# A gated mix of two long convolutions: 640 matmuls that nobody reads near the start, and a new written-out order of all engines

## The chip, the cores and the metric

The kernel runs on one core of a Trainium2 chip. The metric is the device time of one execution in microseconds (us): the median of several runs. A profile of one execution comes with it, taken on the chip, with the start and the duration of every instruction.

## What is computed

Two sequence layers share the input `u` (2048 steps, 448 channels, bf16), and a gate mixes them.

```python
g = sigmoid((u * gate_w).sum(-1, keepdims=True))
K = einsum("dn,dnl,dn->dl", C, exp(dt * A * l), dt * B).real   # 256 complex modes per channel
a = irfft(rfft(u) * rfft(K)) + u * Dskip                       # layer A, length 4096, first 2048 kept
k_shift = sum over t of shifted k * shift_k[:, t]              # four taps
kv = k_shift * v
b = u * (irfft(rfft(kv) * rfft(ssm_k)) + kv * ssm_D)           # layer B
out = g * a + (1 - g) * b
```

## The kernel before

The Fourier transforms are done as matmuls. The 448 channels are worked in four groups of 112 (28 columns in each of four strips of partitions, `H` = 0 to 3), for the two layers A and B. A transform has three forward steps: `spread` (tiles `ps_c`, moved from PSUM into `zs` or `zsK`), `transform` (tiles `ps_2`, which the profile shows as `ps<-zs,s_W`, moved into the same tile), and two multiplications of spectra on VectorE (`products`, which write `zs` and `zsS`). Back again go `stage_a` (matmuls `ps_a` with the table `sa_R`, moved into `U`) and `stage_b` (matmuls `ps_b` with the table `sb_G`).

The kernel `K` of layer A is made on the chip, in eight blocks (class `KGen`, `block(j)` for j = 0 to 7). ScalarE makes powers of the modes (`Tables.levels` and `reals`: Exp and Sin into `ET`), one set for two blocks. VectorE multiplies them out into two tiles, `kg_TQ` and `kg_TP`. When these are complete, 224 small matmuls go into `pk`, and the copy `kg_S`, the gathering matmuls `ps_g`, the copy `kg_KT`, a `spread` and a `transform` follow. In all there are 5,387 matmuls, each with its own weight load.

PSUM holds three buffers under the tag `ps` for all of `ps_v`, `ps_m`, `ps_c`, `ps_2`, `ps_a` and `ps_b`, so a matmul group can start only when the group three before it has been moved out. The moves out are mostly ScalarE's (`evac`).

In the first 45 us the loads arrive, ScalarE and VectorE make the tables (`s_W`, `sb_G`, `sa_R`, `Wc`), and the four-tap sum of `k` runs in eight pieces: VectorE writes `kvt`, eight matmuls of 448 columns add up in `ps_v`, ScalarE copies to `kt`. `sa_R` comes from four phase rows on VectorE, one Sin on ScalarE, and one scaling on VectorE (`Consts.stage_a`).

What sets the order: `Order` records every engine call in program order without issuing it. `ORDER` is a written-out string of call numbers, and `Order.issue` issues the calls in that order, with an order-only dependency between neighbours on one engine. So the queue of each of the five engines, SyncE's DMA issues and GpSimd's index rows among them, is fixed by this string, and every instruction in the profile carries one line, L146. Readers of the profile go by tile names. Tiles are named below with their buffer numbers where several of a name must be told apart, such as `zsK_296`. They are the names in the built program.

Of the kernel before, what the change touches and what calls it, by code (L numbers as in the profile page):

```python
# [41 lines left out]
    "604 23 166 27 73 65 26 31 576 1 75 164 525 74 24 36 76 171 194 192 172-173 198 193 25 35 188 177 174-175 195 582 "  # L42
    "189 580 176 0 34 199 581 201 162 593 160 33 163 594 161 190 165 595 588 167 2 168 577 32 597 178 169 606 602 29 "
    "22 16 191 17 179 21 12 38 13-14 18-19 15 181 186 10 28 180 182 8 170 20 9 3 187 6 183 37 11 7 5 4 30 536 534 528 "
    "526 184 42 79 68 529 185 527 46 535 39 537 544 47 542 196 545 531 197 44 550 202 200 590 583 552 45 543 541 584 "
    "596 589 48 585 591 100 40 530 41 55 533 43 586 101-108 592 603 587 72 67 599 598 49 110 51-52 538 66 90 50 56 "
    "234-241 69 77 532 54 120 53 109 64 242 70 63 215-222 78 80 539 62 243-250 71 540 225-232 61 223 549 224 233 "
    "121-128 130 548 203 546 204 131-138 150 129 547 111-118 551 139-140 600 151-158 119 553 601 554 251 141-148 159 "
    "557 252-259 267 149 319-326 260 327 302-317 556 285-300 318 261 91-98 301 262 555 205-212 81-88 213 99 214 263 "
    "268-283 264 89 265 1110 284 266 574 367 474 346-353 575 366 1111 472 578 471 481 1108 365 354 1109 476 502 473 "  # L50
    "607 364 470 469 468 475 494 561 579 570 565 573 558 566 559 517 563 516 569 478 518 490 512 503 507 498 477 513 "
    "487 489 479 482 519 491 608-635 493 480 483 492 495 486 484 387-402 488 499 496 500 508 1126 522 497 501 485 521 "
    "504 524 370-385 523 514 2488 505 509 636-663 515 506 510 664-691 520 1124 511 1113 692-719 386 1127 1115 1114 "
    "1116 560 421-428 1122 1117 1120 567 403 1129 1119 562 820-835 1131 571-572 1118 720 568 1112 564 429 1852 1121 "
    "721 803-818 2495 2510 2489 2499 2491 1133 2493-2494 2496 1123 2492 722 2490 1135 337-344 836 57 60 59 58 723 "
    "1125 2497 1141 404-419 819 724 345 725 355-362 2511 2498 1137 420 786-801 605 1128 363 777-784 1138 802 328-335 "
    "1130 1140 785 743-758 336 1132 430-437 1142 759-775 1134 1143 438 1464-1479 776 1136 457-464 1851 1139 1853 2500 "
    "1272-1335 1854 1862 837-844 1855 1857 1336-1367 465 1208-1271 2501 2503 2502 845 1856 2504 1480 369 368 2505 "
    "2520 1481-1496 2519 2512 1858 1515-1522 2521 960-967 1859 1144-1207 2506 2513 2523 1497 2514 2522 2515 1861 968 "
    "2524 448-455 1860 2516 439-446 1368 1864 1863 456 1369-1385 2517 2508 2507 2518 1865 969-976 1867 1386 447 1866 "  # L60
    "1387-1426 1869 977 1868 942-949 466 1427 726-741 950 1446-1451 2525 1498-1513 1870 742 2526 1848 1872 1514 1849 "
    "467 924-931 1847 932 906-913 1846 2509 1874 914 863-878 2542 2529 1877 2527-2528 897-904 2543 1523 1875 879-895 "
    "2545 1876 905 933-940 2530 2544 915-922 2563 896 2534 2531 2537 2562 2532 2538 1662-1669 923 2564 1850 2533 2565 "
    "941 1871 1644-1651 1670 1460 951-958 2566 1873 2535 846-861 1461 2569 1652 2536 1878 959 2202-2217 862 2568 1880 "
    "2218 978-1041 1879 2539 1452 1881 2555 2949-2964 1453-1458 2540 2074-2105 1463 2554 2556 2550 1043-1106 "
    "2557-2558 1462 2561 2546 2541 1882-1945 1459 2965 1107 2552-2553 2549 1042 2559 1437-1444 2551 1584-1599 2560 "
    "2573 1445 2567 2548 2966-2981 2547 1600 1428-1435 6194 3968 1618-1633 1436 2570 2982 1653-1660 2571 1946-2009 "
    "1661 2572 2574 1634 2010-2073 2577 3976 3994 3973 3988 1635-1642 3974 3987 3971 2576 2219-2234 2579 3975 2575 "
    "3977 3332 2581 1643 1601-1616 3995 3972 2583 3970 2106 2585 2578 1524-1539 2235 2588 2580 1617 3331 2125-2164 "
    "3333-3334 1575-1582 3969 2165 2582 1558-1573 1583 1540 3335 2107-2123 2584 1541-1556 1574 3337 1671-1678 2590 "  # L70
    "2124 2236-2251 1557 3338 2184-2189 1679 2589 1716-1779 2190 2199 3336 2252 2166-2173 2198 2591 3996 2983-2998 "
    "3339 1707-1714 1780 2174 3997 3000-3007 2999 3982 3341 2191-2196 3983 1715 2586 1698-1705 2197 2253-2260 3340 "
    "3008 3984 2587 1689-1696 1706 3343 2175-2182 2592 2261 1680-1687 1697 2322-2329 4008 3346 2785-2816 1688 "
    "2721-2784 4009 3348 2330 3985 3350 2183 2201 2593-2656 2200 2920-2927 2349-2356 2928 2657-2720 2357 3352 3354 "
    "3342 4010 2262-2277 3357 3345 2817 3344 4011 3989 3347 2818-2834 4012 2340-2347 4023 2278 4000 2313-2320 3999 "
    "4022 2348 3349 3156-3163 4024-4025 3351 2321 1781-1844 3164 4043 3353 4001 4014 2835 4013 2938-2945 4002 4015 "
    "3060-3067 3978-3979 2946 1845 2836-2875 3980 3043-3058 3990-3991 3068 3981 3992 4004 4016 2279-2294 3986 4003 "
    "3993 4005 4018 4042 2296-2311 3998 3355 3059 4044 3356 2295 2331-2338 3358 2312 3026-3041 4045 2876 3360 "
    "2929-2936 2339 2895-2900 4006 3361 4007 2909 3682-3697 2937 4017 4046 2910 4019 3359 2358-2421 4029 4047 "
    "3426-3489 4038 4020 4040 4050 4039 4037 2422 4021 4041 3362-3425 4030 4049 4031 3042 4048 3554-3585 4053 4052 "  # L80
    "4026 4034 4051 4032 4027 6197 4036 4033 2911-2918 4035 3490-3553 4028 4054 2919 5388 4057 3699-3714 3698 4812 "
    "2948 3733-3740 3586 3715 3138-3145 3741 2947 3129-3136 3146 3009-3024 5395 5390 3716-3731 5397 5402 5394 4056 "
    "5410 2901 5403 3025 4055 4059 2902-2907 4058 2908 4811 3174-3181 3732 4060 2886-2893 5411 4813 4062 5391 "
    "2423-2486 3137 4061 5393 5396 4064 5389 3811-3818 4063 2894 4069 3182 2877-2884 5392 2487 3069-3084 3819 4814 "
    "2885 3147-3154 3085 4070 3120-3127 3587-3603 3155 4815 3192-3199 4071 3604 4818 4446-4461 3200 4065 4820 "
    "3605-3644 5404 4068 4817 3103-3118 4066 3645 5399 3128 5398 3655-3662 4067 5400 3086-3101 5405 3663 4072 3119 "
    "3671-3676 5407 4265-4296 4816 3102 4732-4747 3677 5401 5412 4819 3802-3809 4748 5408 3646-3653 5414 4073-4136 "
    "4822 4821 5406 5413 4462 3678-3679 4823 3829-3836 4201-4264 5415 3654 4826 3837 6200 3165-3172 3664-3669 5416 "
    "4137-4200 4828 3810 5429 4830 3173 5428 5417 4832 5418 3183-3190 4824 4297 4825 4766-4773 4827 3191 3201-3264 "
    "4829 4774 3681 3670 5409 3820-3827 3265 5424 4298-4314 5423 4749-4764 3680 4315 5425 4463-4478 3828 4765 "  # L90
    "4316-4355 5426 4831 4409-4416 4479 3266-3329 5419 4833 4356 5420 4417 4839 5421 4838 5458 4480-4487 4382-4387 "
    "5422 4429-4444 4840 5457 5443 5427 5442 5459 5444-5445 3330 5463 5462 4835 4488 4391-4398 4388-4390 3793-3800 "
    "5455 5464 4836 4399 4357-4364 4834 5460 4841 4418-4425 5461 4445 4837 5473 5034-5065 5452 5465 5447 4842-4905 "
    "4426 6195 4970-5033 5448 5466 5454 5433 4365 5468 5456 5469 5451 5450 5467 5453 5446 5449 4375-4380 4400-4407 "
    "5430 5434 5470 4715-4730 6196 4906-4969 4408 5431 5437-5438 4731 5475 3759-3774 4428 4381 5066 5439 4366-4373 "
    "4802-4809 5476 5435 4427 4374 4810 5085-5124 5432 3776-3791 5125 5850 5472 3801 5471 3775 5067-5083 4549-4556 "
    "5436 5474 5084 4506-4521 5440 4557 5477-5478 5441 5151-5156 3742-3757 5479 3792 5480 5849 5482 5157 4567-4574 "
    "3758 5135-5142 5851 5484 4575 3838-3901 5486 4522 5490 5143 4540-4547 3902 4523-4538 5487 4548 5481 5144-5149 "
# [533 lines left out]
def body(  # L632
# [20 lines left out]
    nc = Order(tc)  # L653
# [169 lines left out]
    V.tensor_scalar(out=sel_d[:], in0=dj[:], scalar1=0.0, scalar2=None, op0=ALU.is_equal)  # L823
    pk = psk.tile([P, 512], f32, name="pk")
    V.memset(pk[:], 0.0)

    kg = KGen(tc, nc, kgp, pk, psk, cons, sel_d, d4, ET)
    KA = [None] * NQG
    XA = [None] * NQG
# [168 lines left out]
```

## Time and profile before

| | |
|---|---|
| median of 7 runs | 295.63 us |
| range of the runs | 294.22 to 296.56 us |
| the profiled execution, its own time | 295.48 us |
| its span, first to last instruction | 293.2 us |
| mean granted TensorE clock | 0.891 |
| VectorE (DVE) busy | 265.4 us, 540 instructions |
| ScalarE (ACT) busy | 253.9 us, 411 instructions |
| TensorE (PE) busy | 212.1 us, 5,387 matmuls |
| GpSimd (POOL) busy | 7.4 us |
| moved by DMA | 21.34 MB |

The page gives, for each engine, busy time as a share of the span, then the span in 40 slices of 7.3 us with the busy share in tenths. PEclk is the TensorE clock that was granted, in tenths of full speed. "PEld" is the weight load of TensorE. In a list of waits, "A <- B" means that A stood idle until B released it, and "<- issue" is idle time for which no wait is recorded.

### The profile page before, as it was taken

To read this page: it belongs to the slowest core of one execution; us is meant where nothing else is said; L and a number is where in the kernel's file an instruction comes from. 1 tells how busy PE (TensorE), PEld (TensorE's weight loads), DVE (VectorE), ACT (ScalarE), POOL (GpSimd) and SP (SyncE) were. 2 spreads that over 40 slices of the span, in tenths; PEclk is the share of its full clock that TensorE was granted. 3 is DMA by queue.
4 is the path that set the end of the run, shared out by engine and by line. 5 is a ranking of instruction groups with operands and counts; after the bars stand their busy time and mean duration, and the time that the engine had idled before them with its cause. 6 is when DMAs were issued, how large, how long until landed. Compare 5 with 4: busy or idle time off the path is not lost.

```text
span 293.2 us, 12044 instructions
## 1 busy us (share of the span) xinstructions
PE 212.1 (72%) x5387; PEld 185.6 (63%) x5387; DVE 265.4 (91%) x540; ACT 253.9 (87%) x411; POOL 7.4 (3%) x43
## 2 busy tenths in 40 slices
PE   0067771658977798988998678879677998589740
PEld 0033451647766687877888568869577897578740
DVE  8998999999999989999999899889999999794950
ACT  4999899999999999999799999989999987537500
POOL 7000000000000100000000000000000000000000
PEclk9995995755988999997999799989799999799965
DMA  7999999340144232031004300320500046000068
GB/s 149 190 190 141 174 166 271 63 64 0 35 97 65 48 83 51 2 79 52 4 4 96 75 9 3 65 67 6 125 4 2 4 93 159 7 6 4 2 119 135
DMA packets 53380, 21.34 MB, mean 73 GB/s; under 512 B 48720, under 2 KB 51664, under 8 KB 53328
## 3 DMA queue, kind: packets, MB, share of 16 engines
q1 hardware_dynamic: 48768, 19.42, 36.1%
q10 hardware_dynamic: 4560, 1.15, 2.1%
q8 instruction: 42, 0.69, 1.0%
q14 instruction: 10, 0.08, 0.1%
HBM read 10.01 MB, written 3.21 MB: 45 GB/s over the span
## 4 chain that ended last, share of the span: by engine, by line
ACT 37%; DVE 21%; PE 17%; SPq 9%; issue 6%; DMA 5%; DVEq 0%; ACTq 0%
ACT zs L146 12%; ACT ET L146 9%; SPq L146 9%; DVE kg_P L146 6%; PE pk L146 5%; ACT zsK L146 4%; PE ps_b L146 4%; ACT U L146 3%; PE ps_a L146 3%; PE ps L146 3%; ACT L146 3%; ACT ks_mag L146 3%; DVE kg_TQ L146 3%; DVE zsS L146 3%; DVE ug L146 2%
## 5 line engine op out<-in xcount | busy, mean ns | idle before, releaser
L146 ACT CAST zs<-ps 128x896 bf16<-128x896 f32 x48 | 44.4, 960 | 0.3 <-PE ps L146 0.3
L146 ACT CAST zs<-ps_c 128x1024 bf16<-128x1024 f32 (+1 forms) x48 | 44.2, 942 | 0.0
L146 PEld LDWEIGHTS <-s_W 128*128 128x128 bf16 x544 | 31.9, 106 | 17.2 <-issue 13.7
L146 PE MATMUL pk<-kg_TP,kg_TQ 128*25 128x32 bf16 x1792 | 32.5, 239 | 6.7 <-issue 6.5
L146 DVE TENSOR_TENSOR kg_P<-kg_TQ,ET 128x896 bf16<-128x896 bf16 (+2 forms) x56 | 36.2, 654 | 0.5
L146 PE MATMUL ps<-zs,s_W 128*128 128x112 bf16 x384 | 29.4, 227 | 7.8 <-ACT zs L146 6.0
L146 PEld LDWEIGHTS <-kg_TQ 128*25 128x25 bf16 x1792 | 28.3, 128 | 9.5 <-issue 7.8
L146 PE MATMUL ps_a<-sa_R,zs 128*128 128x128 bf16 x224 | 32.3, 231 | 2.7 <-ACT zs L146 1.6
L146 PE MATMUL ps_b<-U,sb_G 128*128 128x28 bf16 x1024 | 28.3, 175 | 6.1 <-issue 2.6
L146 PEld LDWEIGHTS <-sb_G 128*128 128x128 bf16 x1024 | 27.3, 96 | 7.1 <-issue 4.4
L146 PE MATMUL ps_a<-sa_R,zsS 128*128 128x128 bf16 x224 | 31.6, 229 | 0.0
L146 ACT CAST U<-ps_a 128x1024 bf16<-128x1024 f32 (+2 forms) x30 | 28.0, 963 | 3.8 <-PE ps_a L146 3.8
L146 DVE TENSOR_TENSOR kg_P<-kg_TP,ET 128x1792 bf16<-128x1792 bf16 (+1 forms) x32 | 31.0, 970 | 0.1
L146 PEld LDWEIGHTS <-zsS 128*128 128x128 bf16 x224 | 29.4, 151 | 2.4 <-issue 2.2
L146 PEld LDWEIGHTS <-zs 128*128 128x128 bf16 x224 | 29.3, 151 | 1.8 <-DVE zs L146 0.5
L146 PE MATMUL ps_v<-kvt,scratch 128*128 128x448 bf16 x64 | 15.9, 411 | 16.2 <-DVE kvt L146 14.1
L146 ACT ACTIVATE ET<-ks_ph 128x448 bf16<-128x448 int16 x40 | 23.4, 609 | 0.7 <-DVE kg_P L146 0.7
L146 DVE TENSOR_TENSOR kg_TQ<-kg_P 128x448 bf16<-128x448 bf16 (+2 forms) x56 | 23.4, 420 | 0.1
L146 PE MATMUL ps_c<-Wc,kv 128*64 128x128 bf16 x224 | 17.3, 309 | 7.3 <-ACT zs L146 6.5
L146 PEld LDWEIGHTS <-scratch 128*128 128x128 bf16 x65 | 6.9, 110 | 23.7 <-issue 15.8
L146 PEld LDWEIGHTS <-kv 128*64 128x64 bf16 x224 | 16.0, 218 | 8.4 <-issue 7.5
L146 ACT CAST zsK<-ps_c 128x384 bf16<-128x384 f32 (+2 forms) x27 | 21.0, 779 | 0.0
(103 smaller groups left out, 458.5 us busy)
## 6 DMA issues: line engine op xcount, KB each, us to landing
zsS<-zs SPq DMA_DIRECT2D x16, 448.0 KB, 5.2
kt<-in_B_k_dram SPq DMA_DIRECT2D x16, 112.0 KB, 4.0
vt<-in_B_v_dram SPq DMA_DIRECT2D x4, 448.0 KB, 6.7
skraw<-in_B_ssm_k_dram SPq DMA_DIRECT2D x16, 112.0 KB, 3.6
uu<-in_A_u_dram SPq DMA_DIRECT2D x4, 448.0 KB, 8.8
xfd<-ks_hold SPq DMA_DIRECT2D x2, 672.0 KB, 5.1
ks_xf<-xfd SPq DMA_DIRECT2D x3, 336.0 KB, 3.2
out_dram<-ug SPq DMA_DIRECT2D x8, 112.0 KB, 4.3
```

What stands on the lines that cost most here:

```text
L146: ins = f(*args, **kw)
```

## The change

Part one adds matmuls behind the line that clears `pk`. Each multiplies 128 weight columns of `sa_R` with 64 other columns of it and writes the last 64 columns of the bank of `pk`, which nothing reads. There are 20 times 32 of them.

```diff
     pk = psk.tile([P, 512], f32, name="pk")
     V.memset(pk[:], 0.0)
 
+    for _ in range(20):
+        for i in range(32):
+            nc.tensor.matmul(pk[:, 448:512], lhsT=R[:, 0:128], rhs=R[:, 128:192], start=True, stop=True)
+
     kg = KGen(tc, nc, kgp, pk, psk, cons, sel_d, d4, ET)
```

Part two replaces the whole string `ORDER`. The new calls carry the numbers 605 to 1244 and stand in 40 groups of 16, some of them side by side. Every call behind them in program order has a number that is 640 higher than before. The beginning of the string, old and new:

```diff
-    "604 23 166 27 73 65 26 31 576 1 75 164 525 74 24 36 76 171 194 192 172-173 198 193 25 35 188 177 174-175 195 582 "
...
+    "604 26 525 34 23 27 198 190 576 164 25 33 2 1 166 73 24 36 11 194 10 192 186 8 195 0 35 9 193 187 12 196 14 188 "
...
+    "529 602 177 537 31 527 39 590 161 542 4 162 168 597 167 530 534 68 20 163 5 204 595 165 65 535 605-620 29 577 75 "
+    "169 552 581 541 38 171 550 170 621-636 172 42 582 173 603 175 583 540 174 76 41 584 178 637-652 43 653-668 543 "
...
```

In the built program the new matmuls stand on TensorE as 240 ahead of everything else, 48 behind the first `ps_m` group, 112 in five groups of 16 and one of 32 among the `ps_v`, `ps_m` and `ps_c` groups that follow, 160 behind the last `ps_c` group of the first spectrum, and 80 more two `ps_c` groups later, ahead of the 112 matmuls of the gate. No other instruction is added to TensorE, VectorE, GpSimd or SyncE. ScalarE has 15 loads of its function table where it had 13. The sequences of all five engines differ.

## Prediction

> **What bounds the kernel now.** I read the busy rows and slices of the page first, then the busy time by stretch, then each engine's timeline and the waits.
>
> ```profile
> PE 212.1 (72%) x5387; PEld 185.6 (63%) x5387; DVE 265.4 (91%) x540; ACT 253.9 (87%) x411; POOL 7.4 (3%) x43
> ...
> PE   0067771658977798988998678879677998589740
> ...
> DVE  8998999999999989999999899889999999794950
> ACT  4999899999999999999799999989999987537500
> ...
> PEclk9995995755988999997999799989799999799965
> ```
>
> ```profile
> 0.00:45.00 45.00, 22.44 (x177) 12.81 (x177) 41.81 (x99) 39.40 (x43) 5.70 (x40) 0.92 1.13 168
> 45.00:80.00 35.00, 21.60 (x488) 19.44 (x490) 33.95 (x88) 34.91 (x73) 0.87 (x2) 0.66 0.38 83
> ...
> 145.00:227.00 82.00, 67.62 (x1850) 61.71 (x1843) 77.82 (x157) 80.65 (x144) 0.00 (x0) 0.94 0.18 41
> 227.00:254.00 27.00, 22.95 (x729) 21.01 (x727) 27.00 (x48) 21.30 (x29) 0.00 (x0) 0.99 0.32 72
> 254.00:284.00 30.00, 23.59 (x755) 22.20 (x751) 21.74 (x29) 14.63 (x20) 0.00 (x0) 0.90 0.10 20
> ```
>
> The columns are the stretch, its length, and the busy time of PE, PEld, DVE, ACT and POOL, then clock, DMA share, GB/s. ACT is full from 45 to 227 us and DVE from 45 to 254. PE is not: from 45 to 80 us it runs at 0.66 of its clock and ACT still idles only 0.09 us. A colder or warmer PE there moves nothing. From 254 us on, no engine is full; a chain through PE, ACT and DVE runs.
>
> I took the time of each instruction from the timeline (start to end, or to the next start where two overlap) and added up each engine's work to any point; the idle time to that point is its clock time less this sum. The point that sets the end is the product on DVE that needs the last move into zsK_296: ACT has done 210.9 us of work at its end, at 219.9 us, so it has idled 9.0 us (3.9 before its first instruction, 1.6 up to 33 us, 3.5 later). DVE starts the product at 220.0 and works on, nearly without a gap, to the last kg_TP of the last block at 254.1: 34.0 us. So the path is 210.9 + 9.0 + 34.0 + 0.2 = 254.1, and the end is 39.1 us later, at 293.2.
>
> ```profile
> 14.14 3.15 PE L146 MATMUL ps_v<-kvt,scratch 128*128 128x448 bf16 x8 [14.14 <-DVE kvt L146]
> ...
> 40.07 1.67 PE L146 MATMUL ps_v<-kvt,scratch 128*128 128x448 bf16 x8 [0.21 <-ACT zs L146]
> ...
> 251.84 1.58 PE L146 MATMUL ps_b<-U,sb_G 128*128 128x28 bf16 x57 [2.58 <-issue]
> ...
> 260.36 1.16 PE L146 MATMUL pk<-kg_TP,kg_TQ 128*25 128x32 bf16 x63 [1.36 <-issue]
> ```
>
> ```profile
> q8 instruction: 42, 0.69, 1.0%
> ...
> L146 ACT ACT_TABLE_LOAD x13 | 16.7, 1283 | 4.0 <-DMA kt<-in_B_k_dram 3.9
> ```
>
> The same eight matmuls take 3.15 us on a cold PE and 1.67 us on a warm one. The pauses marked "issue" stand where an instruction packet lands: 0.69 MB in 42 packets for 10,774 weight loads and matmuls is 256 instructions to a packet.
>
> **What the skill says.** "TensorE: Matmul & The Clock Gate", Part 1, has PE at half clock until about 3.4 us of activity have passed; the halves of 3.15 and 1.67 us agree, and the clock row falls to 5 around each lull. "ScalarE: Activation LUTs", What ACT_TABLE_LOAD costs, gives 1283 ns and 1380 ns of drain: the trace has 1283 ns, and no drain, since ACT is busy again at once. "Runtime: NRT & Kernel Launch", Instruction fetch mechanics, has blocks of 256 instructions, fetched while the last one runs and mostly hidden; the packets agree, but 2.58 and 1.36 us at 249 and 259 us are not hidden.
>
> **The change, part by part.**
>
> *The 640 matmuls, price.* No row has 64 columns against 128 weight columns in bf16. From below, ps_b (28 columns) runs at 1.58/57, some 28 ns apiece. From above, transform's 112 columns start 50 ns apart on a warm PE and 94 on a cold one. I take 30 warm and 53 cold.
>
> *240 of them first.* They wait for sa_R, which the new order makes first: ACT's table load ends at 5.1, the Sin takes 0.4, and DVE's scaling is ready at about 6.5. With 3.4 to 6.8 us cold (64 to 128 matmuls) and the rest warm they end at 15 to 17 us. The first kvt, which they stand before, ends on DVE at 16: its place is 1.2 us later than before in DVE's work, and POOL now makes a 512-wide row (0.6 us), smaller ones and a clearing ahead of c_pidx, for which DVE waits some 0.75 us. ACT asks for the first ps_m at 19.5 and for the first ps_v at 22.6 (before: 20.3 and 19.6). So all 240 lie in idle PE time. If that cover fails, by half clock throughout (240 x 53 = 12.7) and a fetch pause of 2.6, PE is at 22 instead of 17 and ACT waits.
>
> *The other 400* stand before ps_h, ps_m and ps_c groups which wait for one of three PSUM buffers anyway; following buffer by buffer, only one wait is left, 0.8 us at the ps_v just before the last ps_c. The 160 end at 46.4 when kv is ready on DVE (46.2); the 80 end before gwt is. Nothing on the path.
>
> *What a warm PE saves.* Up to 45 us ACT lost 0.27 us to ps_v, 0.83 to DVE's sb_ph (itself behind 0.86 for ps_v) and 0.49 to s_ph. Against the 0.8 that remains I get ACT's second Exp load at 42.8 instead of 43.6: -0.8 us. Bounds: -1.7 (no wait) and +3 (cover gone).
>
> *Two more table loads.* ACT now changes to Sin and back within three instructions, after 105 us of its work, for the one phase tile ks_ph_293. 2 x 1.28 = +2.6 us on an engine that is full there. At the joint above, the work sums are: ACT to the last move into zsK_296 209.9 (before 210.9), DVE from there 37.2 (before 34.0), in all 247.1 against 244.9: +2.2 us. The earlier joint at zs_329 reads 246.9 against 244.2. These moves carry the table loads in them. Cover: ACT's 3.5 us of scattered waits after 33 us, if the order closes them. I take them as they are, since they stand by PE pauses and late phases that no order names. Bounds: -1.2 (all closed: 2.2 - 3.4) to +2.7.
>
> *SP and POOL.* The B_im and A_re loads come earlier, the last kt is 20th instead of 23rd, dB 32nd instead of 30th, d4 22nd; xfd moves ahead of the reload of skraw_193, and the last uu stays 41st. The readers of dB and uu (a ps_c group at 31 us, the gate at 50) wait for PSUM and gwt longer than for these. Zero; with the next DMA later, 1 us at most.
>
> *The tail.* The seventh block's kg_TQ is complete 2.4 us later in DVE's work, so its 224 pk matmuls end at about 246 instead of 242.8, if the last kg_TP is kept at 254.1. But 1280 instructions are five packets exactly, so packets now end at known matmuls: not inside the ps_b group that stood 2.58 us. Following PSUM buffers, the last pk group starts at 255.1 instead of 256.4, has 16 fewer transforms behind it, and loses the same 1.3 us to a packet: kg_S at 261.0 instead of 261.6. From there the new order of ps_a, ps_c and ps_b again needs 16.7 us to the last ps_b. So -0.5; bounds -2.6 (pause gone and nothing late) and +2.4 (the late kg_TQ in full).
>
> **Sum.** -0.8 + 2.2 - 0.5 = +0.9 us on the profiled execution: 295.48 + 0.9 = 296.4. Its own time is 0.15 under the median of 295.63, so I say 296.5. The span would be 294.1.
>
> **Rivals.**
>
> A: the new order closes ACT's waits. After 33 us these are 3.5 us; if 1 us is left and the tail brings 1 us instead of 0.5, the sum is 0.9 - 2.5 - 0.5 = -2.1, 293.5. It turns when ACT idles less than some 6.5 us up to the joint (9.0 now). For it: ACT and DVE are so nearly full that each order must be well balanced, and the late pause goes. Against it: 2.6 us more of ACT's work.
>
> B: nothing that can be measured. DVE's 265.4 us are the same, the new matmuls are hidden, and gains and losses cancel: 295.6. For it: the sum of parts is small. Against: every queue is permuted, and pauses of 1 to 3 us will fall elsewhere. About 0.3%, 0.9 us, is what a measurement of this kernel can tell from none.
>
> C: the front fails. The DMA engines are fullest in the first 15 us, and PE must fetch its second packet there. If the 240 stay cold and stand once, ps_v is 4 to 5 us late and ACT with it: 300. Against it: ACT has 2 us in hand.
>
> **Chances.** The forecast, slower by some 1 us, 0.40; A 0.37; B 0.15; C 0.08. The forecast's own spread (+0.2 to +3) puts part under 0.3%. Faster 0.38, same 0.18, slower 0.44. Its own range is 295.8 to 298.5. The whole: down to 291.5 (ACT's waits closed and the pause gone: 0.9 - 3.4 - 2.1 = -4.6), up to 300.5 (C).
>
> **What would show it.** PE starts near 6.5 us and is warm from 10 to 13 us; 240 matmuls end before 17. ACT's second Exp load starts near 42.8. 15 table loads of 1283 ns. The last kg_TP on DVE ends near 255, the last kg_S starts near 262. I am wrong if ACT's idle time up to its last zsK_296 move is under 7 us, or if PE has not begun ps_v by 18 us.

## The result and the profile after

The changed kernel takes 1.0074 times as long as before (95% interval 1.0054 to 1.0093), which is 2.2 us on 295.63, or 297.8 us. The ratio counts, for each kernel, only the executions within 1.5% of its fastest; the changed kernel spreads without a gap from 295.5 to 301.2 us, ten of its 27 runs fall outside, and the medians of all runs, 299.18 us beside 295.91, lie 3.3 us apart. The profiled execution takes 298.21 us, with a span of 296.0 (before: 293.2). So it is slower, as forecast, and 1.3 us above the 296.5 that I named.

The page of the changed kernel, in the lines that answer to those of before:

```profile
PE 229.6 (78%) x6027; PEld 205.2 (69%) x6027; DVE 266.1 (90%) x540; ACT 256.8 (87%) x413; POOL 9.9 (3%) x43
...
DVE  7999999999959999999999999899999999982960
ACT  3999999999979899999999999999999994927500
...
PEclk9999999956977799999999879998979997979985
...
q8 instruction: 47, 0.77, 1.1%
...
L150 PE MATMUL pk<-sa_R 128*128 128x64 bf16 x640 | 21.9, 197 | 7.8 <-DVE sa_R L150 7.5
...
L150 ACT ACT_TABLE_LOAD x15 | 19.2, 1283 | 4.1 <-DMA kt<-in_B_k_dram 3.9
```

PE has 17.5 us more work, ACT 2.9, DVE 0.7. The clock row starts full and the 640 matmuls cost 21.9 us of PE. ACT has 15 table loads of the same 1283 ns. The instruction queue (q8) has 47 packets instead of 42. The busy time by stretch (stretch, length, PE, PEld, DVE, ACT, POOL, clock, DMA share, GB/s) shows where it went wrong; the last line is of the kernel before:

```profile
0.00:45.00 45.00, 33.93 (x660) 26.40 (x661) 42.65 (x101) 39.28 (x42) 7.24 (x40) 1.00 1.06 157
...
80.00:145.00 65.00, 52.97 (x1427) 47.51 (x1427) 59.06 (x118) 62.22 (x104) 0.42 (x1) 0.92 0.21 44
```

```profile
80.00:145.00 65.00, 53.85 (x1411) 48.41 (x1407) 63.11 (x125) 63.04 (x107) 0.79 (x1) 0.95 0.26 56
```

Up to 45 us DVE and ACT have done about what they did before. From 80 to 145 us DVE is busy for 59.1 of 65 us; in the kernel before it was busy for 63.1. PE's front is as forecast (start, length, instructions, idle time before them and its releaser):

```profile
7.46 8.04 PE L150 MATMUL pk<-sa_R 128*128 128x64 bf16 x223 [7.46 <-DVE sa_R L150]
...
16.77 1.48 PE L150 MATMUL ps_v<-kvt,scratch 128*128 128x448 bf16 x7 [0.26 <-DVE kvt L150]
```

The 240 end at 16.5 us, and the first `ps_v` group runs warm at once. The loss is here, in the timeline of all engines:

```profile
77.04 1.66 PE L150 MATMUL pk<-kg_TP,kg_TQ 128*25 128x32 bf16 x95
...
82.18 1.67 PE L150 MATMUL pk<-kg_TP,kg_TQ 128*25 128x32 bf16 x97 [3.48 <-issue]
...
84.74 0.91 ACT L150 CAST zs<-ps 128x896 bf16<-128x896 f32 x1 [1.83 <-PE ps L150]
...
86.66 0.67 PE L150 MATMUL pk<-kg_TP,kg_TQ 128*25 128x32 bf16 x32
...
87.39 0.22 DVE L150 COPY kg_TP<-ET 128x224 bf16<-128x224 bf16 x1 [3.03 <-PE pk L150]
```

PE works through the 192 `pk` matmuls of block 0 and stands 3.48 us in the middle of them, with no wait recorded. Behind it ACT waits 1.83 us for a `ps` group, and DVE waits 3.03 us: `kg_TP` has one buffer, so its first write for block 1 must wait until the last 32 `pk` matmuls have read block 0. The trace says what PE stood for. Counted in order, PE's weight loads and matmuls show every pause of PE marked "issue" in both kernels right behind record 193 plus a multiple of 256, where a new instruction packet is needed. When PE enters the 256 instructions of one packet (128 matmuls), the next packet is asked for: that is read from the landings, most of which begin within 1.3 us of such a point. The packet that PE stood for was so asked for at 75.56 us; it begins to land at 79.51, 3.94 us later, and PE goes on 1.31 us after its last byte. In the kernel before, in block 0's `pk` matmuls, these waits were 0.73 and 0.62 us (75.21 to 75.95 and 78.80 to 79.42), and PE did not stand. There `ps_c` groups stand between the `pk` matmuls, and PE worked 3.6 us on a packet:

```profile
76.50 1.17 PE L146 MATMUL pk<-kg_TP,kg_TQ 128*25 128x32 bf16 x64
77.61 0.71 PE L146 MATMUL ps_c<-Wc,kv 128*64 128x128 bf16 x8
78.25 1.63 PE L146 MATMUL pk<-kg_TP,kg_TQ 128*25 128x32 bf16 x96
```

In the changed kernel the 192 stand in a row, and PE is through the packet entered at 75.56 us in 2.9 us. What delays the next packet is, by the times, the first swap, two DMAs of 448 KB. SyncE's issues, first of the kernel before, then of the changed one:

```profile
78.38 1.18 SPq L146 DMA_DIRECT2D zsS<-zs  x2
```

```profile
74.27 1.18 SPq L150 DMA_DIRECT2D zsS<-zs  x2
```

The new order issues the swap 4.1 us earlier against a `pk` group that starts at the same time (76.5 before, 77.0 after). The profile counts the swap (q1) and the packets (q8) against the same 16 DMA engines, and from 75.5 to 79 us of the changed kernel the swap fills them and no packet lands (queue, its DMA packets, MB, share of the 16 engines):

```profile
q1 hardware_dynamic: 125, 0.78, 101.0%
```

In the tail PE stands twice more in the last `pk` group, and `kg_S` follows it:

```profile
258.39 2.13 PE L150 MATMUL pk<-kg_TP,kg_TQ 128*25 128x32 bf16 x128 [0.35 <-issue]
...
262.12 1.41 PE L150 MATMUL pk<-kg_TP,kg_TQ 128*25 128x32 bf16 x80 [1.60 <-issue]
...
263.56 0.54 ACT L150 CAST kg_S<-pk 128x448 bf16<-128x448 f32 x1 [3.95 <-PE pk L150]
```

The last `kg_TP` ends at 257.1 us (before: 254.1), the last `kg_S` starts at 263.6 (261.6), and the span is 2.8 us longer.

### The profile page after: what moved, and what is told of

It reads as the page before. It is cut to its first block, busy times and chain, and to the rows that moved or that the text cites. A ratio compares the mean times of both kernels' runs of the same rounds, so it can differ in the third digit from the quotient of the medians.

```text
span 296.0 us, 13338 instructions
## 1 busy us (share of the span) xinstructions
PE 229.6 (78%) x6027; PEld 205.2 (69%) x6027; DVE 266.1 (90%) x540; ACT 256.8 (87%) x413; POOL 9.9 (3%) x43
## 4 chain that ended last, share of the span: by engine, by line
ACT 49%; DVE 17%; PE 13%; SPq 7%; issue 6%; DMA 3%; DVEq 0%; ACTq 0%
ACT zs L150 18%; ACT ET L150 12%; SPq L150 7%; ACT zsK L150 5%; DVE kg_P L150 4%; PE pk L150 4%; ACT U L150 4%; ACT L150 3%; ACT ks_mag L150 3%; PE ps_a L150 3%; DVE kg_TP L150 2%; DVE zsS L150 2%; DMA vt<-in_B_v_dram 2%; DVE zs L150 2%; PE ps L150 2%
## 5 line engine op out<-in xcount | busy, mean ns | idle before, releaser
L150 ACT CAST zs<-ps_c 128x1024 bf16<-128x1024 f32 (+1 forms) x48 | 43.5, 941 | 0.1
L150 PEld LDWEIGHTS <-s_W 128*128 128x128 bf16 x544 | 33.0, 108 | 14.3 <-issue 11.0
L150 PE MATMUL ps_a<-sa_R,zs 128*128 128x128 bf16 x224 | 33.8, 239 | 6.0 <-ACT U L150 4.1
L150 PE MATMUL pk<-kg_TP,kg_TQ 128*25 128x32 bf16 x1792 | 31.2, 239 | 8.2 <-issue 6.7
L150 PEld LDWEIGHTS <-zsS 128*128 128x128 bf16 x224 | 30.1, 153 | 5.6 <-issue 3.6
L150 PE MATMUL ps_a<-sa_R,zsS 128*128 128x128 bf16 x224 | 33.1, 236 | 0.0
L150 PEld LDWEIGHTS <-zs 128*128 128x128 bf16 x224 | 29.9, 151 | 2.3 <-DVE zs L150 1.1
L150 PE MATMUL pk<-sa_R 128*128 128x64 bf16 x640 | 21.9, 197 | 7.8 <-DVE sa_R L150 7.5
L150 PEld LDWEIGHTS <-sa_R 128*128 128x128 bf16 x640 | 21.0, 101 | 8.7 <-DVE sa_R L150 7.5
L150 ACT ACT_TABLE_LOAD x15 | 19.2, 1283 | 4.1 <-DMA kt<-in_B_k_dram 3.9
L150 PE MATMUL ps_c<-Wc,kv 128*64 128x128 bf16 x224 | 16.6, 301 | 7.4 <-ACT zs L150 7.0
```

The source lines that it names most:

```text
L150: ins = f(*args, **kw)
```

## The experiments

My theory after the result, S: the time is lost at PE's pause within block 0's `pk` group, because a packet is asked for behind the swap's bytes and needed soon after. The rival from my prediction, T: the two table loads are the loss, on a full ACT. A second rival, M: the unread matmuls themselves stand in the way, or their number matters. The kernels ran in four groups (e1 to e4, e5 to e8, e9 to e11, and e12), each on one chip beside the kernel before. Across groups, and with the changed kernel, the ratios are compared.

| kernel | ratio to before | us | PE's pause in block 0's pk | DVE's wait for kg_TP at 85-88 | last kg_TP ends | last kg_S starts |
|---|---|---|---|---|---|---|
| before | 1 | 0 | 0 | 0 | 254.1 | 261.6 |
| changed | 1.0074 [1.0054, 1.0093] | +2.2 | 3.48 | 3.03 | 257.1 | 263.6 |
| e1, 13 loads | 1.0052 [1.0029, 1.0075] | +1.5 | 3.48 | 3.45 | 256.8 | 264.1 |
| e2, before with 15 loads | 1.0077 [1.0049, 1.0104] | +2.3 | 0 | 0 | 257.0 | 262.8 |
| e3, none of the 640 | 1.0066 [1.0037, 1.0094] | +2.0 | 3.24 | 3.19 | 258.1 | 264.4 |
| e4, new front, old rest | 1.0067 [1.0049, 1.0085] | +2.0 | 0 | 0 | 256.1 | 262.4 |
| e5, quarter swap | 1.0039 [1.0012, 1.0066] | +1.2 | 0.27 | 0.48 | 254.6 | 262.4 |
| e6, quarter swap, 13 loads | 0.9997 [0.9976, 1.0018] | -0.1 | 0.50 | 0.48 | 253.2 | 260.4 |
| e7, 544 | 0.9985 [0.9963, 1.0006] | -0.4 | 2.17 | 1.76 | 255.7 | 260.9 |
| e8, new front without the 640, old rest | 0.9985 [0.9959, 1.0010] | -0.4 | 0 | 0 | 254.3 | 260.5 |
| e9, 544, 13 loads | 0.9932 [0.9901, 0.9962] | -2.0 | 2.10 | 0.96 | 252.8 | 258.2 |
| e10, 608 | 1.0187 [1.0140, 1.0233] | +5.5 | 3.36 | 2.75 | 257.2 | 266.6 |
| e11, 32 | 0.9974 [0.9953, 0.9995] | -0.8 | 2.15 | 0.78 | 253.9 | 259.1 |
| e12, before with 96 | 1.0085 [1.0058, 1.0112] | +2.5 | 0.45 | 0 | 256.7 | 263.2 |

The us column is (ratio - 1) x 295.6; the columns right of it are of the one profiled execution of each, from its timeline. That execution lies up to 1.6 us off the median of its kernel (e4 and e9), so small differences between these columns mean little.

**e1: two table loads fewer.** In `ORDER`, the Sin of `ks_ph_293` (call 3175) moves beside that of `ks_ph_294` (3179):

```diff
-2519 2292 3179
+2519 2292 3179 3175
...
-3193-3194 3175 2068-2075
+3193-3194 2068-2075
```

> The changed kernel with one Sin (tile ks_ph_293) issued 16 ACT instructions earlier, beside the Sin of ks_ph_294, so that ACT loads 13 tables and not 15. Theory (the two loads are the loss, on an engine that is full there): 2.6 us less at the joint of ACT and DVE, so about 0.4 us under the kernel before, 295.2 us. Rival (the loss is in the waits of the new order, DVE's 3.0 us at 87 us and its work behind the joint, and the loads are covered): 297 to 298 us, less than 1 us gained.

```profile
L151 ACT ACT_TABLE_LOAD x13 | 16.7, 1283 | 4.2 <-DMA kt<-in_B_k_dram 4.0
```

The loads are gone (the line is from the groups of instructions), and ACT's work up to its last move into `zsK_296` is 2.5 us less. But its idle time up to there is 11.2 us instead of 9.05, the move ends only 0.3 us earlier, and PE's and DVE's waits at 79 to 88 us stand. The gain against the changed kernel is 0.7 us by the ratios, whose intervals overlap. The two loads were for the most part covered: T does not explain the loss alone.

**e2: two table loads more, in the kernel before.**

```diff
-1879 2539 1452 1881 2555
+1879 2555 2539 1452 1881
```

> The kernel before with one Exp (ET, scale 152) issued ahead of the Sin of ks_ph_294, so that ACT loads 15 tables and not 13, and nothing else is moved. Theory: each load is on the path, +2.5 us, 298.1 us. Rival (ACT has cover behind it): +0.5 us or less, 296.1 us.

Here they cost 2.3 us of their 2.6: the last `kg_TP` is 2.9 us later. My price was right where ACT is what ends last; in the changed kernel the pause comes first.

**e3: none of the 640.** The loop and the calls 605 to 1244 are left out:

```diff
-    for _ in range(20):
-        for i in range(32):
-            nc.tensor.matmul(pk[:, 448:512], lhsT=R[:, 0:128], rhs=R[:, 128:192], start=True, stop=True)
```

> The changed kernel's order with the 640 unread matmuls left out and nothing else moved. Theory (they are hidden, and a warm front saves nothing that lasts): within 0.5 us of the changed kernel, 297.8 us. Rival W (a warm PE does help in the front): 0.8 to 1.5 us slower than the changed kernel, 299 us. Rival H (they stand in the way of ps_v, or their instruction fetch does): 1 us faster than the changed kernel, 296.8 us.

As slow as the changed kernel. The first Exp behind the second load of its table starts at 45.2 us instead of 45.0, so a warm PE brings 0.2 us in the front. The pause is there too (PE's timeline):

```profile
82.19 1.67 PE L147 MATMUL pk<-kg_TP,kg_TQ 128*25 128x32 bf16 x97 [3.24 <-issue]
```

It must be, by S: 640 matmuls are 1,280 instructions, five packets exactly, so packets end at the same instructions with or without them.

**e4: the new front, then the old order.** `ORDER` as changed up to call 472, ACT's first Exp behind its second load of the Exp table, then the order of the kernel before; 112 unread matmuls that were left over stand ahead of the next `ps_2` group, and 80 ahead of the gate.

```diff
-1037-1052 472 1053-1068 517 1750 366
+1037-1052 1750 474 1053-1164 346-353 366 1751 472
...
```

> The changed kernel's order up to ACT's second load of the Exp table (43.7 us), with all 640 matmuls, and the order of the kernel before from there. Theory (the front neither gains nor loses, the loss comes later): within 0.5 us of the kernel before, 295.6 us. Rival (the new front hands over a worse state, DVE or PE late): half or more of the loss is there already, 297 us or more.

The expectation failed, by my own placing: at 48 us ACT waits 2.35 us for the `ps_2` group behind the 112, and DVE 3.2 us behind that. It prices unread matmuls that stand ahead of one that is waited for, and says nothing about the front.

**e8: the same, with none of the 640.** It repeats e4 without that fault.

```diff
-    for _ in range(20):
-        for i in range(32):
-            nc.tensor.matmul(pk[:, 448:512], lhsT=R[:, 0:128], rhs=R[:, 128:192], start=True, stop=True)
```

> The changed kernel's order up to ACT's second load of the Exp table, the order of the kernel before from there, and none of the unread matmuls. It repeats the run of the new front without the groups of unread matmuls that stood in PE's way there (2.4 us of ACT waiting for ps_2 at 48 us). Theory (the new front gains and loses nothing by itself): 295.3 to 296.2 us. Rival (the front hands over a late state): 297 us or more, as in that run.

294.96 us, not to be told from the kernel before. The new front is neutral; the loss is made behind 45 us.

**e5: a quarter of the swap's bytes.**

```diff
-def products(nc, X, S, Y, k0=0, k1=32):
+def products(nc, X, S, Y, k0=0, k1=32, both=False):
...
-        nc.vector.tensor_tensor(out=fl(t), in0=fl(t), in1=fl(Y), op=ALU.mult)
+        nc.vector.tensor_tensor(out=fl(t), in0=fl(X if both else t), in1=fl(Y), op=ALU.mult)
...
-    def swapped(zs):
+    def swapped(zs, ks=32):
...
-            nc.sync.dma_start(swap[64 * r:64 * r + 64], zs[64 - 64 * r:128 - 64 * r])
+            nc.sync.dma_start(swap[64 * r:64 * r + 64, 0:ks], zs[64 - 64 * r:128 - 64 * r, 0:ks])
...
-    KB[0] = swapped(KB[0])
+    KB[0] = swapped(KB[0], 8)
...
-    term0 = products(nc, *KB[0], XB[0])
+    term0 = products(nc, *KB[0], XB[0], both=True)
```

> The changed kernel with the first swap (zsS, two DMAs at 74.3 us) cut to a quarter of its bytes; what it leaves out is the swapped copy, so that the first term's product for zsS is made from zs instead, by a DVE instruction of the same size. Theory S (the instruction packet that PE asks for at 75.6 us lands 3.9 us later behind the swap's bytes, in the middle of block 0's pk group, and DVE's 3.0 us and ACT's 1.8 us of waiting follow from that pause): the packet lands about 1.1 us after it is asked for, the pause falls from 3.5 to 1 us or less, DVE's wait ahead of kg_TP at 87 us to under 1 us, and the time by 1.5 to 2.5 us, to 295.5 to 296.5 us. Rival (the pause comes from the group's own speed, 256 instructions in 3 us, or the lost time returns at the next joint): under 0.5 us gained, 297.5 us or more.

```profile
78.93 1.66 PE L151 MATMUL pk<-kg_TP,kg_TQ 128*25 128x32 bf16 x97 [0.27 <-issue]
...
84.81 0.22 DVE L151 COPY kg_TP<-ET 128x224 bf16<-128x224 bf16 x1 [0.48 <-PE pk L151]
```

PE enters the packet at 75.55 us, as in the changed kernel, but the next one now lands 1.13 us later instead of 3.94. From 75.5 to 79 us the DMA queues now show the packet and a swap that leaves the engines free:

```profile
q1 hardware_dynamic: 153, 0.22, 29.3%
q8 instruction: 1, 0.02, 1.8%
```

The pause falls from 3.48 to 0.27 us, DVE's wait from 3.03 to 0.48, ACT's 1.83 is gone, and the last `kg_TP` ends 2.5 us earlier. The other kernels agree: with the whole swap and the same packet ends the packet landed 3.92 us (e1) and 3.50 us (e3) after it was asked for, with the quarter 1.23 us (e6). That is S shown, for this one pause. The time gains only 1.0 us, less than I expected, and the two intervals overlap: in this run a packet of the tail, asked for at 251.42 while the last swap runs, lands 3.3 us later, PE stands 1.99 us where it stood 0.35, and 1.4 of the 2.5 us are lost again before `kg_S`.

**e6: both.** The edits of e5 and e1.

> The same with the Sin of ks_ph_293 beside that of ks_ph_294 as well, so that ACT loads 13 tables. Theory S with the loads behind it (in the changed kernel ACT waits for a DVE that the pause made late, so a shorter ACT gains little; without the pause ACT counts again): 1.5 to 2.5 us faster than with the quarter swap alone, 293.5 to 294.5 us. Rival (DVE's work behind the joint is the bound either way): within 0.6 us of the quarter swap alone, some 296 us.

1.2 us faster than e5, less than expected and more than the rival allows, though the intervals overlap: without the pause the loads count again, for about half of their 2.6 us. With both edits the kernel is as fast as before, its interval clear of the changed kernel's: together the pause and the loads are the size of the loss. Which of them is the larger the runs don't tell: alone, the smaller swap gained 1.0 us and the fewer loads 0.7.

**e7: 544 instead of 640.** The calls 605 to 700 go, all of the first 240, and what follows is numbered down.

```diff
-    for _ in range(20):
+    for _ in range(17):
```

> The changed kernel with 544 unread matmuls instead of 640, all 96 taken from the first group of 240, so that each packet of 256 instructions ends 64 matmuls before or after where it did. Theory S: the packet asked for at 73.2 us lands ahead of the swap, the next one still behind it, and PE stands after block 0's large pk group instead of within it, for some 2 us instead of 3.5: 1 to 1.5 us faster than the changed kernel, 296.5 us. Rival (the place of the packets' ends does not matter): within 0.5 us of the changed kernel, 297.8 us.

```profile
77.01 3.09 PE L151 MATMUL pk<-kg_TP,kg_TQ 128*25 128x32 bf16 x191
...
82.27 0.21 PE L151 MATMUL pk<-kg_TP,kg_TQ 128*25 128x32 bf16 x1 [2.17 <-issue]
...
86.08 0.22 DVE L151 COPY kg_TP<-ET 128x224 bf16<-128x224 bf16 x1 [1.76 <-PE pk L151]
```

Now 191 of the 192 run through, PE stands at the next packet's end for 2.17 us, and DVE waits 1.76. The time falls by 2.6 us against the changed kernel, more than the 1 to 1.5 expected: in the tail, too, the packets end elsewhere, and `kg_S` follows the last `kg_TP` by 5.2 us instead of 6.4.

**e9: 544 and 13 loads.** The edits of e7 and e1.

> The run with 544 unread matmuls, and the Sin of ks_ph_293 beside that of ks_ph_294 (13 table loads). Theory (once PE's pause within block 0's pk group is shortened, ACT's two loads count for some 1.4 us, as they did with the quarter swap): 1.0 to 1.5 us faster than with 544 alone, 293.4 us, under both kernels. Rival (DVE alone sets the joint, the loads stay hidden): within 0.5 us of 544 alone, 294.7 us.

As expected, and faster than both kernels: 0.9932, with an interval that ends at 0.9962. The loads are worth 1.6 us here.

**e10: 608.** Two groups of the first 240 go.

```diff
-    for _ in range(20):
+    for _ in range(19):
```

> The changed kernel with 608 unread matmuls, 32 fewer in the first group. Theory (what counts is where a packet of 128 matmuls ends, not how many unread ones there are): the packet's end moves from the 95th to the 127th of block 0's 192 pk matmuls, its request at some 76.9 us is still behind the swap's bytes, PE stands for about 3.2 us within the group, and the time is that of the changed kernel, 297.8 us. Rival (fewer unread matmuls make it faster, 96 fewer having gained 2.6 us): about 0.9 us faster than the changed kernel, 296.9 us.

The expected 297.8 us was missed by 3.3. At block 0 the expectation holds: the packet, entered at 76.93, lands at 80.14, PE stands 3.36 us after 127 matmuls, and the last `kg_TP` ends at 257.2 as in the changed kernel. The tail I had left out:

```profile
261.89 2.13 PE L151 MATMUL pk<-kg_TP,kg_TQ 128*25 128x32 bf16 x128 [2.57 <-issue]
...
266.59 0.53 ACT L151 CAST kg_S<-pk 128x448 bf16<-128x448 f32 x1 [6.20 <-PE pk L151]
```

There a packet entered at 255.69 lands 3.5 us later, PE stands 2.57 and 1.60 us within the last `pk` group, and `kg_S` starts 3.0 us later than in the changed kernel, in all 5.5 us slower than before. 32 unread matmuls fewer make it slower, 96 fewer make it faster: M in the form of "fewer is better" falls.

**e11: only 32.** All others go; packets end where they do with 544.

```diff
-    for _ in range(20):
+    for _ in range(1):
```

> The changed kernel's order with only 32 unread matmuls, all in the first group: the packets end where they do with 544 (the difference of 512 is four packets). Theory (place is all): the time of the run with 544 within 0.5 us, 294.9 us, though the order without any unread matmul took 297.6 us. Rival (it was a warm PE, or the number of unread matmuls, that made the run with 544 faster): as without any, 297.6 us.

The time of e7, as expected, with the pause at the same instruction (191 run through, then 2.15 us). Against e3 the 32 matmuls bring 2.7 us. M falls; what is left is the place of the packets' ends.

**e12: the kernel before, with 96 unread matmuls ahead of all.**

```diff
     V.memset(pk[:], 0.0)
 
+    for i in range(96):
+        nc.tensor.matmul(pk[:, 448:512], lhsT=ident, rhs=ident[:, 0:64], start=True, stop=True)
```

> The kernel before, its order untouched, with 96 unread matmuls of the identity ahead of all others on PE (in its idle time up to 14 us), so that every packet ends 96 matmuls earlier in the program. Theory (where packets end counts in this kernel too): its pauses of 2.7, 1.5, 2.6 and 1.4 us at 163, 194, 249 and 259 us are gone or under 1 us, and it is 1 to 2.5 us faster, 293.1 to 294.6 us. Rival (only the collision of the new order with its first swap matters; the pauses of the kernel before lie beside other work): within 0.5 us of the kernel before.

It missed with the sign: 2.5 us slower. That the ends of packets count in this kernel too holds, but I could not say where. The pauses at 163, 194, 250 and 260 us are only smaller (1.60, 1.03, 1.50 and 0.88 us), and a new one stands within block 6's `pk` group:

```profile
245.11 0.98 PE L147 MATMUL pk<-kg_TP,kg_TQ 128*25 128x32 bf16 x50 [2.16 <-issue]
...
246.12 0.53 ACT L147 CAST kg_S<-pk 128x448 bf16<-128x448 f32 x1 [3.48 <-PE pk L147]
246.13 0.22 DVE L147 COPY kg_TP<-ET 128x224 bf16<-128x224 bf16 x1 [1.37 <-PE pk L147]
```

For it DVE waits 1.37 us ahead of the last block's `kg_TP`. Another of 1.74 us stands behind block 0's `pk` group at 85 us. I had worked from the times of an execution without these pauses, with 0.7 us from request to landing; 2.1 to 3.4 us were measured for the four packets with the longest pauses. Part of the loss may have another cause: from 9 to 30 us PE's mean clock is 0.51 here (0.84 before), and ACT's first Exp behind its second load is already 0.5 us late.

## Why the prediction was right or wrong

*Sign and size.* Slower was forecast, by 0.9 us; it is 2.2. The time that the ratio gives, 297.8 us, lies within the range. The loads, my whole reason for the sign, are worth 0.7 us (e1), or 1.2 where the pause is gone (e6), not 2.2, and the other cause that the runs found stood in the sum at zero. So the sign is right in part by luck. One slip besides: the lower end of the whole range, 291.5, is 291.0 by its own sum (295.6 - 4.6).

*The 640 matmuls: right as to cover.* 223 of them took 8.0 us, 36 ns each, between my 30 and 53; PE started at 7.5 us, was warm from 10.5, and had finished them at 16.5. e3 shows all 640 hidden.

*What a warm PE saves, -0.8: wrong.* The second Exp load starts at 43.74 us, before at 43.62. ACT did lose less to `ps_v` and `s_ph`, but 1.03 us newly at 6.6 us, for `sb_ph`. I had named DVE's wait for `c_pidx` (0.71 us measured) and not who waits for DVE behind it. That the one follows from the other is only read from the order; no run took it away. e3 puts the warm PE at 0.2 us at that point, e8 the new front at nothing that can be measured.

*Two more table loads, +2.2: right in the kernel before, too much in the changed one.* There they cost 2.3 us (e2), here 0.7 (e1), and 1.2 and 1.6 where the pause is gone or shorter (e6, e9). I took ACT's waits up to the joint "as they are", 9.0 us, and 9.05 were measured; but that is chance. The 3.5 us of scattered waits did go, mostly those of 1.23 and 0.67 us behind 141 us, and 1.83 and 0.75 us came at 85 and 98 us, the first behind the pause. And idle time is not a constant that adds to work: with the loads taken out it grew by 2.2 us (e1), since ACT then waited for engines that the pause had made late. I had summed along ACT and left out that DVE came to the joint with 2.8 us less work done than before (207.0 against 209.8) and 2.1 us more idle time.

*SP and POOL, zero: this is the step whose mechanism failed.* I followed the loads, `dB`, `uu` and `xfd`, and asked who reads them. I did not see that the first swap is issued 4.1 us earlier beside PE's largest group, nor that a DMA can cost time through what is queued behind it for another engine. "Runtime: NRT & Kernel Launch" in the Trainium skill, Instruction fetch mechanics, calls the crossing from block to block mostly hidden, and so it is for all but 5 of the 47 packets here; the one that cost most waited behind the swap's bytes. The trace of the kernel before had it already: the packets asked for at 160.31, 190.22 and 245.92 us, each 1.1 to 2.5 us behind the issue of a swap's second DMA (158.10, 187.71, 244.79), began to land 2.20, 2.53 and 3.07 us later, and for these PE stood its 2.71, 1.48 and 2.58 us. I had seen packets and pauses, and wrote under rival B that "pauses of 1 to 3 us will fall elsewhere", without place, price or a bound in the sum. The missing term is 2.5 us at the last `kg_TP`, of which 1.0 us is left in the time (e5).

*The tail, -0.5: right in sign.* From the last `kg_TP` to the end it took 38.8 us instead of 39.1. The pause in `ps_b` is gone as forecast, but PE stands 0.35 and 1.60 us in the last `pk` group, for which I had 1.3, and 1.30 at block 6.

*The rivals.* A is what the new order does where the pause is felt less: I let it turn when ACT idles less than some 6.5 us up to the joint, and in e11, where DVE waits 0.78 us instead of 3.03, ACT idles 6.3 us and the kernel is 0.8 us faster than before. C did not happen: `ps_v` began at 16.8 us.

*Open.* That packets land late behind a swap's bytes is shown at one place (e5, e6), and its size there; at the other places, the tail, e12 and the kernel before, it is read from the times alone. No run kept the whole swap and moved only its issue 4.1 us back, or only broke up the row of 192 `pk` matmuls, so how the loss divides between these two sides of the new order is not shown. e7 and e11 are alike in packets, and DVE waits 1.76 and 0.78 us: behind the pause the same 16 `ps_c` matmuls took 1.06 us in e7 and 0.64 in e11, and PE's mean clock from 80 to 90 us was 0.83 in the one and 1.00 in the other. These are single executions, what decides the clock was not tried, and some of e9's gain over e7 in the profiled execution (DVE's 0.96 against 1.76) is of this kind.

## What to carry to other kernels

When instructions are moved, count PE's instruction packets as transfers: find where each ends in the program, what DMA is in flight when the next is asked for, and whether PE needs it within some 3.5 us, or 6.6 behind a swap as here. A row of small matmuls that holds a whole packet runs into the next one's landing. In a kernel such as this a difference of 1% between two orders is no verdict on the orders before some matmuls that nothing reads, from 32 to 96 here, have been put in front to shift the packets. And the idle time of an engine must not be carried over as a constant: ask for each wait what would come last if it closed.

## What the runs showed of the hardware

- A packet of 256 PE instructions began to land some 1.1 us after PE had entered the packet before it at 75.55 us with a short swap, and 3.94 us after with a swap of twice 448 KB under way. The landing took 0.9 to 1.6 us, and PE went on 1.2 to 1.8 us after it in every pause marked "issue" that was longer than 0.25 us.
- 128 `pk` matmuls run for 2.1 to 2.2 us, less than the 3.5 us that went from the entry at 242.34 us to PE going on in the changed kernel. So a row of them that holds a whole packet costs a pause of about 1.3 us even with no swap near (1.30 us there). In e7, where only one packet's end lies within the 224 of block 6, they ran through without a pause from 240.73 to 244.34 us.
- In the new order 0, 32, 544, 608 and 640 unread matmuls gave +2.0, -0.8, -0.4, +5.5 and +2.2 us against the kernel before.
- 96 matmuls that ended at 6.5 us did not keep PE warm: the first `ps_v` group at 14.1 us took 3.14 us, as in the kernel before.
